# Transposing Q, K and x with the DMA crossbar instead of the matrix engine, from the third chunk on

## The chip, the cores and the metric

The kernel runs on one core of a Trainium2 chip. The metric is the device time of one execution in microseconds, as the median of three runs. The engines are named as in the profile: PE is TensorE's matmuls and PEld its weight loads, DVE is VectorE, ACT is ScalarE, POOL is GpSimd, and SP is SyncE, on whose queue the ordinary loads, the stores and (after the change) the transposing transfers are issued.

## The reference

A gated linear attention for 4 batches of 8 heads, 768 steps and 48 channels per head is followed by a mixture of four dense experts on 3,072 rows of 384 numbers:

```python
f = 1.0 / (1.0 + np.exp(-f_logit))
for t in range(S):
    state = f[:, :, t, :, None] * state + np.einsum('bhd,bhe->bhde', k[:, :, t], v[:, :, t])
    y[:, :, t] = np.einsum('bhd,bhde->bhe', q[:, :, t], state)
x = attn_out.transpose(0, 2, 1, 3).reshape(B * S, H * D)
p = domain_probs / (domain_probs.sum(-1, keepdims=True) + 1e-09)
for e in range(E):                       # E = 4, w1: 384 x 1024, w2: 1024 x 384
    h = np.maximum(x @ w1[e], 0.0)
    out += p[:, e:e + 1] * (h @ w2[e])
```

## The kernel before

**Tiling.** The 768 steps are cut into six chunks (c = 0 to 5) of 128 steps. For each chunk and each of the four batches (b), the attention part runs as a chain of steps, written here as the kernel names them with c.b behind:

- gate1, gate2 (ACT): softplus of the gates, for two batches at a time from chunk 1 on. cs (PE, L244 and L247): cumulative sums of the gates by a matmul. exps (ACT, L251 to L254): both exponentials of them.
- q, k, v: products of q and k with the exponentials (L257) and a cast of v (L261). From chunk 2 on they run on POOL alone, before that on POOL or DVE.
- tpq, tpk (PE, L265): four transposes each, of two heads at a time, into one bank of PSUM; ev_tp (L214 on DVE, tile QK) copies both to SBUF.
- at (PE, L273): eight products of K and Q, transposed; ev_at0 and ev_at1 (DVE, L277) mask them into AT.
- y (PE, L284 and L288): the chunk's output from the state and from AT; ev_y (L212 on ACT or L214 on DVE, tile yb) rounds it to bf16.
- xt (PE, L313): three transposes of yb; ev_xt (L212 or L214, tile xT) copies them into xT, the experts' input.
- kv (PE, L294), ev_kv (DVE, L301) and state (POOL, L308, L309) carry the state to the next chunk.

The experts then work on a chunk's 512 rows: h (PE, L317) is three matmuls of w1 with xT for one of eight blocks of 128 hidden units of one expert, relu (L325 on ACT or L323 on DVE) takes it out of PSUM, o (PE, L329) is four matmuls with w2, and ev_o (L336, L338) adds the result to the output tile, which store (L344) writes to memory. In chunk 1 the first two experts are done in halves of 256 rows, so an h there is three matmuls of 256 columns.

**What sets the order.** Each step is an Op with a cost per engine, a priority, the steps it depends on and the buffers it takes and frees. Plan.run places the steps one after the other on five lanes (PE, ACT, DVE, POOL, and one lane called DMA) as soon as their inputs and buffers are there by the plan's own costs, by priority. The instructions are then issued in that order on each engine, and it stays fixed: if a transfer comes later than planned, the engine that is to use it waits, and everything behind it on that engine waits too. Attention for chunk c + 1 is planned between the experts' steps for chunk c. The loads of chunk c + 2 are placed in the same stretch, on the lane DMA, which is SP's queue: SP issues loads and stores in order, and an issue that waits for its data or for its buffer holds back all those behind it.

**Buffers that matter here.** Two PSUM banks hold h's (ps_h: 2), so the third h in a row can't start until the relu of the first is done. Two buffers hold QK, two yb and two xT. Four PSUM banks (ps_t) serve all attention steps.

Of the kernel before, what the change touches and what calls it, by code (L numbers as in the profile page):

```python
# [97 lines left out]
def kernel(  # L98
# [45 lines left out]
    ones = const.tile([T, 1], BF16)  # L144
    nc.gpsimd.memset(ones, 1.0)
    pads = {}
    for nm, nb in (("gp", 2), ("qp", 1), ("kp", 1)):
# [25 lines left out]
    for nm, a in (("f", f_logit), ("q", q), ("k", k), ("v", v)):  # L173
# [12 lines left out]
    def tl(kind, *key):  # L186

        if (kind, key) not in tiles:
            room = kind if kind in rooms else "ps_t"
            slot = P.slot[(room, kind) + key if room == "ps_t" else (room,) + key]  # L190
            if room in ("gp", "qp", "kp"):
# [15 lines left out]
    def hh(b, n=1):  # L207
        return slice((b % 2) * H, (b % 2 + n) * H)
# [45 lines left out]
            nc.scalar.activation(out=tl("egs", c, b), in_=cs[0:MP, HD:HD + NP], func=AF.Exp, scale=-1.0)  # L254

    def product(c, b, j, eng):
        engines[eng].tensor_tensor(out=tl(("qp", "kp")[j], c, b)[:, 0, :, 0:D], in0=tl("qk"[j], c, b // 2)[:, hh(b), :],  # L257
                                   in1=tl("e", c, b)[:, j].rearrange("t (h d) -> t h d", d=D), op=ALU.mult)

    def cast_v(c, b, eng):  # L260
# [1 line left out]

    def pe_tp(c, b, j):
        for i in range(NP):
            nc.tensor.transpose(out=tl("tp", c, b)[:, j, i, :], in_=flat(tl(("qp", "kp")[j], c, b)[:, 0], i)[:, 0:MP],  # L265
                                identity=ident)

    def pe_at(c, b):
        QK = tl("QK", c, b)
# [10 lines left out]
    def pe_y(c, b):  # L280
        y, AT, vb, QK = tl("y", c, b), tl("AT", c, b), tl("vb", c, b), tl("QK", c, b)
        for i in range(NP):
            if c > 0:
                nc.tensor.matmul(out=y[:, i * 2 * D:(i + 1) * 2 * D], lhsT=QK[:, 0, i, :],  # L284
                                 rhs=Sb[c % 2][:, b, i, :], start=True, stop=False, skip_group_check=True)
            for r in range(2):
                h = 2 * i + r
                nc.tensor.matmul(out=y[:, h * D:(h + 1) * D], lhsT=AT[:, r, i, :], rhs=vb[:, h, :],  # L288
                                 start=(c == 0), stop=True, skip_group_check=True)

    def pe_kv(c, b):
        kp, vb = tl("kp", c, b)[:, 0], tl("vb", c, b)
        for i in range(NP):
            nc.tensor.matmul(out=tl("KV", c, b)[0:MP, i * 2 * D:(i + 1) * 2 * D], lhsT=flat(kp, i)[:, 0:MP],  # L294
                             rhs=flat(vb, i), start=True, stop=True)
# [78 lines left out]
    def attention(c, slot, gran):  # L374
        G = {}
        more = c < C - 1
        for b0 in range(0, B, gran):
            p, d, half = slot(b0, 0) - 0.5, 0.54 if gran == 1 else 0.84, b0 // 2
            g1 = P.add(f"gate1 {c}.{b0}", {"ACT": d}, lambda e, b0=b0: gate1(c, b0, gran), p,
                       deps=[ld[c, "f", b0]], takes=[("ex", c, b0)], frees=[("f", c, half)])  # L380
            g2 = P.add(f"gate2 {c}.{b0}", {"ACT": d}, lambda e, b0=b0: gate2(c, b0, gran), p + 0.1,
                       deps=[g1], takes=[("gp", c, half)], frees=[("ex", c, b0)])
            for b in range(b0, b0 + gran):
                G[b] = g2
        for b in range(B):
# [10 lines left out]
            qm = P.add(f"q {c}.{b}", pe, one(product, 0), s(4) - 0.2,  # L396
                       deps=[ex, ld[c, "q", b]], takes=[("qp", c, b)], frees=[("q", c, half), ("e", c, b)])
            km = P.add(f"k {c}.{b}", pe, one(product, 1), s(4) - 0.1,
                       deps=[ex, ld[c, "k", b]], takes=[("kp", c, b)], frees=[("k", c, half), ("e", c, b)])
            vb = P.add(f"v {c}.{b}", {"POOL": 0.5, "DVE": 0.36} if c < 2 else {"POOL": 0.5}, one(cast_v), s(4),  # L400
                       deps=[ld[c, "v", b]], takes=[("vb", c, b)], frees=[("v", c, half)])
            tq = P.add(f"tpq {c}.{b}", {"PE": 0.22}, on(pe_tp, 0), s(4), deps=[qm],
                       takes=[pt_("tp")], frees=[("qp", c, b)], lag=0.2)
            tk = P.add(f"tpk {c}.{b}", {"PE": 0.22}, on(pe_tp, 1), s(4) + 0.01, deps=[km],
                       takes=[pt_("tp")], frees=[("kp", c, b)], lag=0.2)
            et = P.add(f"ev_tp {c}.{b}", {"DVE": 0.69}, lambda e, b=b: copy(e, tl("QK", c, b), tl("tp", c, b)), s(4) + 0.1,
                       deps=[tq, tk], takes=[("QK", c, b)], frees=[pt_("tp")])
# [9 lines left out]
            xt = P.add(f"xt {c}.{b}", {"PE": 0.17}, on(pe_xt), s(13), deps=[ey],  # L417
                       takes=[pt_("xp")], frees=[("yb", c, b)], lag=0.2)
            xdone[c, b] = P.add(f"ev_xt {c}.{b}", {"ACT": 0.48, "DVE": 0.4},
                                lambda e, b=b: copy(e, tl("xT", c)[:, :, b * T:(b + 1) * T], tl("xp", c, b)),  # L420
                                s(13) + 0.1, deps=[xt], takes=[("xT", c)], frees=[pt_("xp")])
            if more:
                kv = P.add(f"kv {c}.{b}", {"PE": 0.22}, on(pe_kv), s(15), deps=[km, vb, y],
                           takes=[pt_("KV")], frees=[("vb", c, b), ("kp", c, b)], lag=0.2)
# [110 lines left out]
```

## Time and profile before

| What | Value |
|---|---|
| median of 3 runs | 324.24 us (322.96 to 326.19) |
| the profiled execution: its own time | 324.19 us |
| the profiled execution: its span | 322.5 us |
| PE busy | 306.1 us, 95% of the span |
| ACT, DVE, POOL busy | 169.1, 142.1 and 92.6 us |
| clock granted to PE | 1.00 |
| median time from issue to landing: store of 192 KB, loads of 384 KB | 1.9 us; 5.6 to 6.0 us |

The profiled execution's time lies 1.7 us above its span and within 0.05 us of the median, so the span can stand for the runs. A matmul's duration in the trace (for example 0.38 us) is longer than the distance to the next matmul's start, since they overlap; what a step costs PE is read from the distance of starts.

### The profile page before, as it was taken

What the parts mean: (1) busy time and instruction counts of PE and PEld (TensorE: products, weight loads), DVE (VectorE), ACT (ScalarE), POOL (GpSimd) and SP (SyncE); (2) the same over time, 40 slices, a digit from 0 to 9 for tenths busy, and PEclk for the clock granted to TensorE, in tenths of its full rate; (3) what the DMA queues carried; (4) which work ended last, traced back from release to release, by engine and by line L of the source; (5) the groups of instructions that cost most, each with busy time, mean ns of one, the idle gap of its engine ahead of it and who ended that gap; (6) DMA issues with size and microseconds to landing.
All of it is one profiled execution on the core that took longest, in us unless ns stands there. A gap on an engine that the chain in (4) does not pass through costs nothing.

```text
span 322.5 us, 5781 instructions
## 1 busy us (share of the span) xinstructions
PE 306.1 (95%) x2304; PEld 181.3 (56%) x2304; DVE 142.1 (44%) x271; ACT 169.1 (52%) x326; POOL 92.6 (29%) x160
## 2 busy tenths in 40 slices
PE   1979999998999999999999999999999999999995
PEld 1753455566877655555555556555555555555552
DVE  5690002399888533214653343654343543201223
ACT  5634754654767675556434455443455444465440
POOL 4695000047997800001423222423322200000000
PEclk9999999999999999999999999999999999999999
DMA  7999999999999994510400200000100000200002
GB/s 155 205 149 191 198 208 209 203 191 207 205 224 220 190 203 94 138 58 2 98 2 0 75 24 2 0 2 0 68 33 3 0 2 0 73 26 0 0 2 98
DMA packets 111531, 30.31 MB, mean 94 GB/s; under 512 B 102800, under 2 KB 109968, under 8 KB 111504
## 3 DMA queue, kind: packets, MB, share of 16 engines
q1 hardware_dynamic: 105744, 23.65, 36.7%
q0 software_dynamic: 5760, 6.29, 11.7%
q8 instruction: 18, 0.29, 0.4%
q14 instruction: 9, 0.07, 0.1%
HBM read 31.51 MB, written 4.72 MB: 112 GB/s over the span
## 4 chain that ended last, share of the span: by engine, by line
PE 89%; DVE 6%; issue 1%; ACT 1%; DMA 1%; DVEq 0%; ACTq 0%
PE ps_h L317 40%; PE ps_o L329 37%; PE ps_t L265 3%; PE ps_t L273 2%; DVE AT L277 2%; PE ps_t L288 1%; PE ps_t L244 1%; PE ps_t L313 1%; DVE kp L257 1%; PE ps_t L284 1%; PE ps_t L294 1%; PE ps_t L247 1%; DMA f<-in_f_logit_dram 1%; DVE QK L214 1%; DVE o L336 1%
## 5 line engine op out<-in xcount | busy, mean ns | idle before, releaser
L325 ACT ACTIVATE h<-ps_h 128x512 bf16<-128x512 f32 (+1 forms) x182 | 104.2, 573 | 114.1 <-PE ps_h L317 108.2
L317 PE MATMUL ps_h<-xT,w_sb 128*128 128x512 bf16 (+1 forms) x624 | 158.2, 367 | 0.7 <-ACT xT L212 0.6
L329 PE MATMUL ps_o<-w_sb,h 128*128 128x384 bf16 x768 | 154.1, 326 | 0.0
L329 PEld LDWEIGHTS <-h 128*128 128x128 bf16 x768 | 71.5, 98 | 53.1
L336 DVE SCALAR_TENSOR_TENSOR o<-ps_o,pn,o 128x384 f32<-128x384 f32 x72 | 44.4, 616 | 103.5 <-PE ps_o L329 102.3
L317 PEld LDWEIGHTS <-w_sb 128*128 128x128 bf16 x624 | 60.1, 99 | 49.2 <-issue 4.6
L277 DVE TENSOR_TENSOR AT<-ps_t,mask 128x512 bf16<-128x512 f32 x48 | 31.1, 684 | 19.9 <-PE ps_t L273 19.7
L261 POOL CAST vb<-v 128x384 bf16<-128x384 f32 x20 | 10.5, 539 | 90.5 <-PE ps_t L294 47.9
L257 POOL TENSOR_TENSOR qp<-q,e 128x384 bf16<-128x384 f32 x21 | 21.2, 1014 | 40.8 <-ACT e L251 37.1
L308 POOL TENSOR_TENSOR Sf<-Sf,egs 48x192 f32<-48x192 f32 x40 | 20.3, 508 | 20.5 <-DVE Sf L301 18.6
L323 DVE TENSOR_SCALAR h<-ps_h 128x512 bf16<-128x512 f32 (+1 forms) x26 | 14.9, 577 | 20.2 <-PE ps_h L317 15.3
L214 DVE COPY QK<-ps_t 112x1024 bf16<-112x1024 bf16 x24 | 16.5, 686 | 16.5 <-PE ps_t L265 16.5
L257 POOL TENSOR_TENSOR kp<-k,e 128x384 bf16<-128x384 f32 x19 | 19.2, 1014 | 5.2 <-ACT egs L254 4.1
L301 DVE TENSOR_TENSOR Sf<-Sf,ps_t 48x192 f32<-48x192 f32 x40 | 14.0, 349 | 6.7 <-PE ps_t L294 6.0
L338 ACT ACTIVATE o<-ps_o,pn 128x384 f32<-128x384 f32 x23 | 13.4, 581 | 5.8 <-PE ps_o L329 5.3
L251 ACT ACTIVATE e<-ps_t 128x384 f32<-128x384 f32 x24 | 11.8, 491 | 7.4 <-DVE AT L277 3.4
L309 POOL CAST sb<-Sf 48x192 bf16<-48x192 f32 x40 | 13.6, 339 | 2.6
L288 PE MATMUL ps_t<-vb,AT 128*128 128x48 bf16 x192 | 12.5, 190 | 1.5 <-DVE AT L277 1.4
L244 PE MATMUL ps_t<-gp,Ub 128*128 128x384 bf16 x24 | 8.5, 355 | 5.4 <-ACT gp L240 4.9
L288 PEld LDWEIGHTS <-AT 128*128 128x128 bf16 x192 | 10.5, 101 | 3.7 <-DVE AT L277 2.1
L265 PE MATMUL ps_t<-ident,kp 128*112 128x128 bf16 x96 | 10.4, 236 | 2.2 <-DVE kp L257 2.2
L252 ACT ACTIVATE e<-ps_t 128x384 f32<-128x384 f32 x24 | 11.8, 494 | 0.0
(48 smaller groups left out, 182.3 us busy)
## 6 DMA issues: line engine op xcount, KB each, us to landing
w_sb<-in_moe_w_dram POOLq DMA_DIRECT2D x8, 768.0 KB, 21.5
out_dram<-o SPq DMA_DIRECT2D x24, 192.0 KB, 1.9
k<-in_k_dram SPq DMA_DIRECT2D x10, 384.0 KB, 5.6
f<-in_f_logit_dram SPq DMA_DIRECT2D x10, 384.0 KB, 5.8
q<-in_q_dram SPq DMA_DIRECT2D x10, 384.0 KB, 5.8
v<-in_v_dram SPq DMA_DIRECT2D x10, 384.0 KB, 6.0
f<-in_f_logit_dram SPq DMA_DIRECT2D x4, 192.0 KB, 3.7
k<-in_k_dram SPq DMA_DIRECT2D x4, 192.0 KB, 3.9
```

Of the source, the lines that this page charges most:

```text
L214: engines[eng].tensor_copy(out=out, in_=in_)
L257: engines[eng].tensor_tensor(out=tl(("qp", "kp")[j], c, b)[:, 0, :, 0:D], in0=tl("qk"[j], c, b // 2)[:, hh(b), :], in1=tl("e", c, b)[:, j] ...
L265: nc.tensor.transpose(out=tl("tp", c, b)[:, j, i, :], in_=flat(tl(("qp", "kp")[j], c, b)[:, 0], i)[:, 0:MP], identity=ident)
L277: nc.vector.tensor_tensor(out=tl("AT", c, b)[:, r].rearrange("s i t -> s (i t)"), in0=tl("A", c, b, r).rearrange("s i t -> s (i t)"), in1= ...
L288: nc.tensor.matmul(out=y[:, h * D:(h + 1) * D], lhsT=AT[:, r, i, :], rhs=vb[:, h, :], start=(c == 0), stop=True, skip_group_check=True)
L301: nc.vector.tensor_tensor(out=Sf[rows, b], in0=Sf[rows, b], in1=KV[rows, :, r, :], op=ALU.add)
L308: nc.gpsimd.tensor_tensor(out=Sf[rows, b], in0=Sf[rows, b], in1=eg, op=ALU.mult)
L317: nc.tensor.matmul(out=tl("ps_h", c, e, fc, n0)[:, n0:n1], lhsT=w1_sb[:, e, kk, fc * 128:(fc + 1) * 128], rhs=tl("xT", c)[:, kk, n0:n1], s ...
L323: nc.vector.tensor_relu(out=dst, in_=src)
L325: nc.scalar.activation(out=dst, in_=src, func=AF.Relu)
L329: nc.tensor.matmul(out=tl("ps_o", c, e, nt)[:, 0:Din], lhsT=tl("h", c, e)[:, fc, nt * T:(nt + 1) * T], rhs=w2_sb[:, e, fc, :], start=(fc = ...
L336: nc.vector.scalar_tensor_tensor(out=o, in0=op, scalar=pe, in1=o, op0=ALU.mult, op1=ALU.add)
```

## The change

From chunk 2 on (16 of the 24 pairs of chunk and batch) the steps tpq, tpk and ev_tp become one step tp: a transposing transfer on SP's queue that reads the products of q and k (128 x 1024 bf16, 256 KB) from one SBUF tile and writes QK. The steps xt and ev_xt become one transposing transfer of 96 KB from yb into xT. For this, q's and k's products share a tile (qk, 7 of them, in place of 6 qp and 7 kp), and QK has 128 partitions in place of 112. Chunks 0 and 1 keep PE's transposes. The plan is given the new steps on the lane DMA, with a cost of 1.8 and 0.9 and 2.2 more until they count as landed.

```diff
-    rooms = {"ps_h": 2, "ps_o": 2, "ps_t": 4, "f": 4, "q": 4, "k": 4, "v": 4, "ex": 2, "gp": 4, "e": 2, "qp": 6, "kp": 7,
+    rooms = {"ps_h": 2, "ps_o": 2, "ps_t": 4, "f": 4, "q": 4, "k": 4, "v": 4, "ex": 2, "gp": 4, "e": 2, "qk": 7,
...
+    def dma_tp(c, b):
+        nc.sync.dma_start_transpose(out=tl("QK", c, b).rearrange("m j i t -> m (j i) t"),
+                                    in_=tl("qk", c, b).rearrange("t j h d -> t (j h d)"))
+
+    def dma_xt(c, b):
+        nc.sync.dma_start_transpose(out=tl("xT", c)[:, :, b * T:(b + 1) * T], in_=tl("yb", c, b))
...
+            if c < 2:
+                tq = P.add(f"tpq {c}.{b}", {"PE": 0.22}, on(pe_tp, 0), s(4), deps=[qm],
+                           takes=[pt_("tp")], frees=[("qk", c, b)], lag=0.2)
...
+            else:
+                et = P.add(f"tp {c}.{b}", {"DMA": 1.8}, on(dma_tp), s(4), deps=[qm, km], takes=[("QK", c, b)],
+                           frees=[("qk", c, b)], lag=2.2)
...
+            else:
+                xdone[c, b] = P.add(f"xt {c}.{b}", {"DMA": 0.9}, on(dma_xt), s(13), deps=[ey], takes=[("xT", c)],
+                                    frees=[("yb", c, b)], lag=2.2)
```

With the new steps and costs the plan comes out in another order. Two places matter for what follows. The line numbers of the changed kernel are seven higher from L317 on (h is L324, o is L336, the store is L351).

The first is PE in the experts' half-width stretch of chunk 1, while the attention of chunk 2 is under way. In the kernel before, two h's (in tiles 1573 and 1579) stand in a row, and then comes an attention step, cs:

```order
L317 LDWEIGHTS w_sb
L317 MATMUL ps_h_1573<-xT_927,w_sb 128x256
L317 LDWEIGHTS w_sb
L317 MATMUL ps_h_1579<-xT_927,w_sb 128x256
L317 LDWEIGHTS w_sb
L317 MATMUL ps_h_1579<-xT_927,w_sb 128x256
L317 LDWEIGHTS w_sb
L317 MATMUL ps_h_1579<-xT_927,w_sb 128x256
L244 LDWEIGHTS Ub
L244 MATMUL ps_t_1585<-gp_88,Ub 128x384
```

In the changed kernel the middle of one of its runs of four h's (1349, 1353, 1360, 1366) reads:

```order
L324 LDWEIGHTS w_sb
L324 MATMUL ps_h_1353<-xT_915,w_sb 128x256
L324 LDWEIGHTS w_sb
L324 MATMUL ps_h_1360<-xT_915,w_sb 128x256
L324 LDWEIGHTS w_sb
L324 MATMUL ps_h_1360<-xT_915,w_sb 128x256
L324 LDWEIGHTS w_sb
L324 MATMUL ps_h_1360<-xT_915,w_sb 128x256
L324 LDWEIGHTS w_sb
L324 MATMUL ps_h_1366<-xT_915,w_sb 128x256
```

The transposes that stood between h's are gone and the attention steps that hang on them have moved later. Behind chunk 1's last xt the kernel before has no place with three h's in a row; the changed one has three runs of four.

The second place is SP's queue in the second half of the program. Before, only stores stand there (chunk 3's, then chunk 4's):

```order
L344 DMA out_dram<-o_2603 128x384
L344 DMA out_dram<-o_2636 128x384
L344 DMA out_dram<-o_2684 128x384
L344 DMA out_dram<-o_2725 128x384
L344 DMA out_dram<-o_3198 128x384
L344 DMA out_dram<-o_3231 128x384
```

In the changed kernel the transposing transfers of chunk 5 (QK and xT) stand between chunk 3's last two stores and chunk 4's first:

```order
L269 DMA_TRANSPOSE QK_2953<-qk_104 128x8x128
L351 DMA out_dram<-o_2566 128x384
L351 DMA out_dram<-o_2602 128x384
L269 DMA_TRANSPOSE QK_3029<-qk_92 128x8x128
L273 DMA_TRANSPOSE xT_3089<-yb_3080 128x3x128
L269 DMA_TRANSPOSE QK_3114<-qk_94 128x8x128
L273 DMA_TRANSPOSE xT_3089<-yb_3173 128x3x128
L269 DMA_TRANSPOSE QK_3203<-qk_96 128x8x128
L273 DMA_TRANSPOSE xT_3089<-yb_3255 128x3x128
L273 DMA_TRANSPOSE xT_3089<-yb_3336 128x3x128
L351 DMA out_dram<-o_3021 128x384
```

Each of these transfers now stands in one line with stores that wait for ev_o, and with loads in the stretch before; what they feed (at and h on PE) stands where the plan put it.

More of the change, by code (lines that the diff above doesn't have):

```diff
@@ L146 @@
     pads = {}
-    for nm, nb in (("gp", 2), ("qp", 1), ("kp", 1)):
+    for nm, nb in (("gp", 2), ("qk", 2)):
         for i in range(rooms[nm]):
@@ L190, in tl @@
             slot = P.slot[(room, kind) + key if room == "ps_t" else (room,) + key]
-            if room in ("gp", "qp", "kp"):
+            if room in ("gp", "qk"):
                 tiles[kind, key] = pads[room, slot]
@@ L256, in product @@
     def product(c, b, j, eng):
-        engines[eng].tensor_tensor(out=tl(("qp", "kp")[j], c, b)[:, 0, :, 0:D], in0=tl("qk"[j], c, b // 2)[:, hh(b), :],
+        engines[eng].tensor_tensor(out=tl("qk", c, b)[:, j, :, 0:D], in0=tl("qk"[j], c, b // 2)[:, hh(b), :],
                                    in1=tl("e", c, b)[:, j].rearrange("t (h d) -> t h d", d=D), op=ALU.mult)
@@ L264, in pe_tp @@
         for i in range(NP):
-            nc.tensor.transpose(out=tl("tp", c, b)[:, j, i, :], in_=flat(tl(("qp", "kp")[j], c, b)[:, 0], i)[:, 0:MP],
+            nc.tensor.transpose(out=tl("tp", c, b)[:, j, i, :], in_=flat(tl("qk", c, b)[:, j], i)[:, 0:MP],
                                 identity=ident)
+    def dma_tp(c, b):
[3 more added lines that the diff above has]
+        nc.sync.dma_start_transpose(out=tl("xT", c)[:, :, b * T:(b + 1) * T], in_=tl("yb", c, b))
     def pe_at(c, b):
@@ L283, in pe_y @@
             if c > 0:
-                nc.tensor.matmul(out=y[:, i * 2 * D:(i + 1) * 2 * D], lhsT=QK[:, 0, i, :],
+                nc.tensor.matmul(out=y[:, i * 2 * D:(i + 1) * 2 * D], lhsT=QK[0:MP, 0, i, :],
                                  rhs=Sb[c % 2][:, b, i, :], start=True, stop=False, skip_group_check=True)
@@ L396, in attention @@
             qm = P.add(f"q {c}.{b}", pe, one(product, 0), s(4) - 0.2,
[L397 removed]
+                       deps=[ex, ld[c, "q", b]], takes=[("qk", c, b)], frees=[("q", c, half), ("e", c, b)])
             km = P.add(f"k {c}.{b}", pe, one(product, 1), s(4) - 0.1,
[L399 removed]
+                       deps=[ex, ld[c, "k", b]], takes=[("qk", c, b)], frees=[("k", c, half), ("e", c, b)])
             vb = P.add(f"v {c}.{b}", {"POOL": 0.5, "DVE": 0.36} if c < 2 else {"POOL": 0.5}, one(cast_v), s(4),
                        deps=[ld[c, "v", b]], takes=[("vb", c, b)], frees=[("v", c, half)])
[L402 to L407, printed above, removed]
+            if c < 2:
+                tq = P.add(f"tpq {c}.{b}", {"PE": 0.22}, on(pe_tp, 0), s(4), deps=[qm],
+                           takes=[pt_("tp")], frees=[("qk", c, b)], lag=0.2)
+                tk = P.add(f"tpk {c}.{b}", {"PE": 0.22}, on(pe_tp, 1), s(4) + 0.01, deps=[km],
+                           takes=[pt_("tp")], frees=[("qk", c, b)], lag=0.2)
+                et = P.add(f"ev_tp {c}.{b}", {"DVE": 0.69}, lambda e, b=b: copy(e, tl("QK", c, b)[0:MP], tl("tp", c, b)), s(4) + 0.1,
+                           deps=[tq, tk], takes=[("QK", c, b)], frees=[pt_("tp")])
+            else:
+                et = P.add(f"tp {c}.{b}", {"DMA": 1.8}, on(dma_tp), s(4), deps=[qm, km], takes=[("QK", c, b)],
+                           frees=[("qk", c, b)], lag=2.2)
             at = P.add(f"at {c}.{b}", {"PE": 0.35}, on(pe_at), s(7), deps=[et],
@@ L416, in attention @@
                        deps=[y], takes=[("yb", c, b)], frees=[pt_("y")])
[L417 to L421, printed above, removed]
+            if c < 2:
+                xt = P.add(f"xt {c}.{b}", {"PE": 0.17}, on(pe_xt), s(13), deps=[ey],
+                           takes=[pt_("xp")], frees=[("yb", c, b)], lag=0.2)
+                xdone[c, b] = P.add(f"ev_xt {c}.{b}", {"ACT": 0.48, "DVE": 0.4},
+                                    lambda e, b=b: copy(e, tl("xT", c)[:, :, b * T:(b + 1) * T], tl("xp", c, b)),
+                                    s(13) + 0.1, deps=[xt], takes=[("xT", c)], frees=[pt_("xp")])
+            else:
+                xdone[c, b] = P.add(f"xt {c}.{b}", {"DMA": 0.9}, on(dma_xt), s(13), deps=[ey], takes=[("xT", c)],
+                                    frees=[("yb", c, b)], lag=2.2)
             if more:
                 kv = P.add(f"kv {c}.{b}", {"PE": 0.22}, on(pe_kv), s(15), deps=[km, vb, y],
-                           takes=[pt_("KV")], frees=[("vb", c, b), ("kp", c, b)], lag=0.2)
+                           takes=[pt_("KV")], frees=[("vb", c, b), ("qk", c, b)], lag=0.2)
                 ek = P.add(f"ev_kv {c}.{b}", {"DVE": 0.74}, on(ev_kv), s(15) + 0.1,
```

4 lines of the change are left out of this document (2 added, 2 removed).

## The prediction

> **What bounds the kernel now.** I read the page's engine lines and the shares of the chain that ended last, then the busy times by stretch (behind the stretch's length: PE, PEld, DVE, ACT and POOL busy, with instructions in brackets, then PE's clock, the DMA engines' share, GB/s).
>
> ```profile
> PE 306.1 (95%) x2304; PEld 181.3 (56%) x2304; DVE 142.1 (44%) x271; ACT 169.1 (52%) x326; POOL 92.6 (29%) x160
> ...
> DMA  7999999999999994510400200000100000200002
> ...
> q1 hardware_dynamic: 105744, 23.65, 36.7%
> ...
> PE 89%; DVE 6%; issue 1%; ACT 1%; DMA 1%; DVEq 0%; ACTq 0%
> ```
>
> ```profile
> 80.00:92.00 12.00, 12.00 (x166) 9.95 (x164) 10.50 (x22) 9.15 (x27) 11.37 (x19) 1.00 1.03 206
> 92.00:104.00 12.00, 12.00 (x154) 9.48 (x152) 10.51 (x23) 8.26 (x20) 9.38 (x21) 1.00 1.06 223
> 104.00:116.00 12.00, 12.00 (x105) 7.91 (x104) 6.90 (x12) 7.73 (x17) 7.44 (x11) 1.00 1.17 198
> ...
> 228.00:275.00 47.00, 47.00 (x349) 26.41 (x347) 20.01 (x33) 22.72 (x42) 7.82 (x8) 1.00 0.05 18
> ```
>
> PE is busy 306.1 of 322.5 us at full clock, carries 89% of the chain, and in the stretches where the change acts it is busy for the whole of them. DVE and ACT, which lose copies by the change, are not full there, so what they lose is worth nothing by itself; PE's time is. The DMA engines are full up to about 125 us and nearly idle behind that, so the new transfers first meet loads and later an empty queue.
>
> **What is removed.** The starts on PE in one batch of chunk 4 show what a transpose costs it:
>
> ```profile
> 198.52 0.81 PE L317 MATMUL ps_h<-xT,w_sb 128*128 128x512 bf16 x3
> 199.17 0.39 PE L265 MATMUL ps_t<-ident,qp 128*112 128x128 bf16 x4
> 199.39 0.39 PE L265 MATMUL ps_t<-ident,kp 128*112 128x128 bf16 x4
> 199.61 0.81 PE L329 MATMUL ps_o<-w_sb,h 128*128 128x384 bf16 x4
> ...
> 200.91 0.36 PE L294 MATMUL ps_t<-vb,kp 128*112 128x96 bf16 x4
> 201.11 0.33 PE L244 MATMUL ps_t<-gp,Ub 128*128 128x384 bf16 x1
> ```
>
> ```profile
> 267.03 0.81 PE L329 MATMUL ps_o<-w_sb,h 128*128 128x384 bf16 x4
> 267.30 0.56 DVE L214 CAST yb<-ps_t 128x384 bf16<-128x384 f32 x1 [0.48 <-PE ps_t L288]
> ...
> 269.62 0.33 PE L313 MATMUL ps_t<-ident,yb 128*128 128x128 bf16 x3
> ...
> 269.79 0.81 PE L329 MATMUL ps_o<-w_sb,h 128*128 128x384 bf16 x4
> ...
> 271.74 0.81 PE L317 MATMUL ps_h<-xT,w_sb 128*128 128x512 bf16 x3
> ```
>
> The transposes of Q and K occupy PE from 199.17 to 199.61, 0.44 us; those of x from 269.62 to 269.79, 0.17 us. Per batch that is 0.61 us, and for 16 batches **9.8 us**, all of it on a PE that has other work ready, so all of it is gained unless PE then waits.
>
> **What is added on PE's side: waits for relu.** The kernel has two tiles for h, so a third h in a row waits for the first's relu. After the change three runs of four h's stand in chunk 1's half-width stretch, where there were none. Chunk 0's h's, all in a row, show the price, and a later pair with an o behind it shows the pace without it:
>
> ```profile
> 31.27 1.46 PE ps_h L317 x6
> 32.76 1.46 PE ps_h L317 x6
> ...
> 117.53 1.29 PE ps_h L317 x6
> ```
>
> ```profile
> L325 ACT ACTIVATE h<-ps_h 128x512 bf16<-128x512 f32 x161 | 96.2, 597 | 108.6 <-PE ps_h L317 102.7 <-DVE o L336 3.0 <-DVE Sf L301 0.9
> ...
> L325 ACT ACTIVATE h<-ps_h 128x256 bf16<-128x256 f32 x21 | 8.0, 385 | 5.5 <-PE ps_h L317 5.5
> ...
> L323 DVE TENSOR_SCALAR h<-ps_h 128x256 bf16<-128x256 f32 x11 | 4.6, 422 | 2.8 <-PE ps_h L317 2.6
> ...
> L251 ACT ACTIVATE e<-ps_t 128x384 f32<-128x384 f32 x24 | 11.8, 491 | 7.4 <-DVE AT L277 3.4 <-PE ps_t L247 2.9 <-DVE vb L261 0.9
> ```
>
> ```profile
> 103.93 0.49 PE L317 MATMUL ps_h<-xT,w_sb 128*128 128x256 bf16 x3
> 104.26 0.81 PE L329 MATMUL ps_o<-w_sb,h 128*128 128x384 bf16 x4
> ```
>
> A pair takes 32.76 - 31.27 = 1.49 us there instead of 1.29, a wait of 0.20. It is the relu (0.60) and the matmul's tail and handoffs (0.25) less the next h (0.65). With half the width, h takes 104.26 - 103.93 = 0.33 and relu 0.39 to 0.42, so a wait is 0.39 + 0.25 - 0.33 = 0.3 us; where ACT or DVE is in the middle of another instruction (an exponential, 0.49), up to 0.8. Three runs cost 0.9 to 2.4 us; I take 1.8, since by the windows above DVE is busy for 88% and ACT for 69 to 76% of the stretch from 80 to 104. If relu is always at hand, the cost is nothing.
>
> **What is added: 32 transfers.** PE waits only where a transfer lands later than the place that the fixed order gives its user, so what counts is the cover, the time from a transfer's release to its user.
>
> For xT the tightest place is the chunk's last batch, and the rows above show it for chunk 5: DVE has rounded yb at 267.30 + 0.56 = 267.86, and the next chunk's first h starts at 271.74, or at 271.57 without the 0.17 of transposes. Cover: **3.7 us**. At the turns to chunks 4 and 3 a kv, or a kv and an o, stands there besides, and at the turn to chunk 2 seven o's do.
>
> For QK in chunk 5 these rows count:
>
> ```profile
> 234.34 0.81 PE L329 MATMUL ps_o<-w_sb,h 128*128 128x384 bf16 x4
> ...
> 236.38 1.00 POOL L257 TENSOR_TENSOR kp<-k,e 128x384 bf16<-128x384 f32 x1
> ...
> 244.94 0.40 PE L273 MATMUL ps_t<-QK 48*128 48x128 bf16 x8
> ```
>
> The product of k is ready at 237.38 and its user starts at 244.94, less 0.44 of transposes: 7.1 us of cover, and the other batches of chunk 5 are ordered alike. In chunk 2 it is less, because there are two QK buffers: the transfer of batch 2 waits for y of batch 0, and between that y and the user there now stand three o's and four h's (0.65 each by the starts above, 4.55), one kv (201.11 - 200.91 = 0.20) and one at (0.40 with its tail), 5.0 us or more, **4.8 us** less the handoff. The order has two such places, and up to six more in chunks 2 and 3 whose transfers stand behind loads or stores.
>
> The trace has no transposing transfer, so its price is bounded by other transfers on SP's queue (bytes and time from issue to landing):
>
> ```profile
> out_dram<-o SPq DMA_DIRECT2D x4, 192.0 KB, 2.1
> ...
> q<-in_q_dram SPq DMA_DIRECT2D x1, 384.0 KB, 3.7
> k<-in_k_dram SPq DMA_DIRECT2D x1, 384.0 KB, 4.3
> ```
>
> ```profile
> out_dram<-o SPq DMA_DIRECT2D x8, 192.0 KB, 1.8
> ```
>
> ```profile
> k<-in_k_dram SPq DMA_DIRECT2D x3, 384.0 KB, 6.1
> ```
>
> A store of 192 KB on an empty queue lands in 1.8 us, a load of 384 KB with little before it in 3.7 to 4.3, and a load behind others in 6.1. QK's 256 KB lie between: bounds 1.8 and 6.1; by size alone, between the store and a free load of 4.0, it is 2.5. I take 3.5, nearer to the load, since the loads too move short pieces (the page's queue q1: 23.65 MB in 105,744 packets, 224 bytes each). For xT (96 KB) the bounds are 1.8 and 4.3, since by then little else is in flight, and I take 2.5. Neither exceeds its cover, so these waits are put at **0**. If they land later by e than their covers, PE loses e at each place: two to four turns for xT, about eight places for QK.
>
> [...]
>
> **What moves past SP's queue.** A load or store behind a transfer whose product or buffer is late must wait too. These rows show the room:
>
> ```profile
> 97.02 2.65 SPq L344 DMA_DIRECT2D out_dram<-o  x1
> ...
> 119.70 1.65 SPq L218 DMA_DIRECT2D v<-in_v_dram  x1
> 131.18 0.36 SPq L344 DMA_DIRECT2D out_dram<-o  x1
> ```
>
> ```profile
> 111.44 0.83 ACT L236 ACTIVATE ex<-f 128x768 f32<-128x768 f32 x1
> ```
>
> The fourth store of chunk 0 and the loads behind it were issued from 97.02 on, the last burst at 119.70, and then SP stood still till 131.18. So the loads of chunks 4 and 5 may slip by 10 us; their first user (the gates, at 111.44 and later) runs one chunk ahead of need. In the other direction, a QK of chunk 5 stands behind two stores of chunk 3: the second's o is on PE at 234.34 for 0.81 us in the rows above, so it ends two microseconds before the product of k is ready at 237.4. Both are put at 0.
>
> **Sum.** The profiled execution took 324.2 us (1.7 above its span, and the median of the runs is the same): 324.2 - 9.8 + 1.8 + 0 = **316.2 us**. The start (up to 80 us) and the end (from 275 us, the last expert stages) have no edit in them.
>
> **The rivals.**
>
> *1. Transfers as slow as loads in a full queue (slower).* Mechanism: a transposing transfer lands like a load behind others, QK in 6.1 us and xT in 4.3. For it: in the stretch to 125 us the queue is full and is served in order. Against it: behind 160 us nothing else is in flight. Price: QK exceeds 4.8 by 1.3 at eight places, 10.4; xT exceeds 3.7 by 0.6 at the last two turns, 1.2. Time: 316.2 + 11.6 = 328. It decides from a QK landing of 4.8 + 8.0/8 = 5.8 us on; there the gain of 8.0 is gone.
>
> *2. The gain is eaten (no change).* QK lands in about 5.4 us and the relu waits reach their upper end of 2.4: 324.2 - 9.8 + 2.4 + 8 x 0.6 = 321.6. The bounds of 1.8 to 6.1 allow it and no row excludes it; the room for it is narrow, half a microsecond of landing time.
>
> *3. A transfer that works block by block (much slower).* QK is eight blocks of 128 x 128; if each were handled after the one before it, the landing could be twice that of a load in a full queue, 12.2 us. That exceeds 4.8 at eight places and 7.1 at the other eight, 59 + 41 = 100 us, so about 416. Against it: loads of short packets land in 3.7 to 4.3. [...]
>
> *4. No relu waits, quick transfers.* 314.4.
>
> **How the numbers follow.** About 1% (3.2 us) is what a measurement of this kernel can tell from no change. Forecast and rival 4 together 0.65 (314 to 319), rival 2 0.13, rival 1 0.15, rival 3 0.07. Faster 0.65, same 0.13, slower 0.22. The likeliest case's own range is 314 to 319; to leave out no more than 2 in 10 the range runs from 314 to 330, past rival 1's 328, with rival 3 left out.
>
> **What would show it.** L265 falls from 192 to 64 matmuls and L313 (L320) from 72 to 24. Issue to landing for QK is under 4.8 and for xT under 3.7 us. PE's idle before L273 (L280) and before h at a chunk's turn stays near 0, and new idle on PE before h between 85 and 105 us, released by relu, sums to 1 to 3 us. I am wrong if PE waits for DMA before L280: then the landing times say which rival it was.

## The result and the profile after

The changed kernel took **315.63 us** (median, 315.22 to 315.96) against 323.78 us of the kernel before on the same chip: a ratio of 0.974, with a 95% interval of 0.968 to 0.979. The forecast was 316.2. The profiled execution of after took 315.96 us, its span is 314.1.

The page of after, in the lines that were shown of before (engines' busy time, the DMA engines' busy tenths, SP's transfer queue, the chain's shares):

```profile
PE 295.3 (94%) x2098; PEld 171.1 (54%) x2128; DVE 132.5 (42%) x249; ACT 163.0 (52%) x310; POOL 92.6 (29%) x160
...
DMA  8999999999999087999692113200322200200002
...
q1 hardware_dynamic: 129296, 29.42, 49.2%
...
PE 88%; DVE 7%; issue 2%; ACT 1%; DMA 1%; DVEq 0%; ACTq 0%
```

PE is busy for 10.8 us less than before and still carries 88% of the chain. The new transfers show in q1: 5.8 MB more, in 23,552 more packets. The DMA engines now stay busy to the 21st of the 40 slices (165 us), where they had little to do from the 16th on; in between, the 14th slice (102 to 110 us) has become empty.

The groups of instructions by shape (line, engine, operation, tiles | busy, mean ns of one | idle time of the engine before them and what ended it), and below them the DMA issues (KB where known, median us from issue to landing):

```profile
L324 PE MATMUL ps_h<-xT,w_sb 128*128 128x512 bf16 x498 | 140.5, 385 | 2.2 <-ACT xT L212 0.6 <-issue 0.2
...
L280 PE MATMUL ps_t<-QK 48*128 48x128 bf16 x192 | 10.6, 233 | 1.0 <-DVE QK L214 0.4 <-DVE yb L214 0.4 <-DVE Sf L308 0.2
...
L265 PE MATMUL ps_t<-ident,qk 128*112 128x128 bf16 x64 | 7.2, 268 | 3.5 <-DVE qk L257 2.7 <-ACT xT L212 0.6 <-ACT e L252 0.2
...
L320 PE MATMUL ps_t<-ident,yb 128*128 128x128 bf16 x24 | 3.3, 260 | 0.5 <-DVE QK L214 0.2 <-ACT yb L212 0.2
```

```profile
QK<-qk SPq DMA_TRANSPOSE x16, 3.2
xT<-yb SPq DMA_TRANSPOSE x16, 2.4
```

L265 fell to 64 and L320 to 24 instructions, as announced. PE's idle time before the products that read QK (L280) and before h (L324) is ended by DVE and ACT; no DMA is named. Q and K's transfer lands in 3.2 us, x's in 2.4 (medians; the slowest of the 16 in 4.4 and 3.9).

The turn to chunk 5 in the timeline (start, duration), which the prediction used for x's cover, and the first and the last of the three runs of four h's in chunk 1 (x12 matmuls, or x6 and x6):

```profile
259.02 0.56 DVE L214 CAST yb<-ps_t 128x384 bf16<-128x384 f32 x1 [0.47 <-PE ps_t L295]
...
259.61 1.18 SPq L273 DMA_TRANSPOSE xT<-yb  x1
...
263.31 0.81 PE L324 MATMUL ps_h<-xT,w_sb 128*128 128x512 bf16 x3
```

```profile
90.69 1.82 PE L324 MATMUL ps_h<-xT,w_sb 128*128 128x256 bf16 x12
92.35 1.46 PE L336 MATMUL ps_o<-w_sb,h 128*128 128x384 bf16 x8
...
100.23 0.82 PE L324 MATMUL ps_h<-xT,w_sb 128*128 128x256 bf16 x6
101.44 0.81 PE L324 MATMUL ps_h<-xT,w_sb 128*128 128x256 bf16 x6 [0.39 <-DVE h L330]
102.09 1.46 PE L336 MATMUL ps_o<-w_sb,h 128*128 128x384 bf16 x8
```

yb is ready at 259.58, the transfer lands at 262.0 (2.4 later), and h starts at 263.31: 1.3 us to spare. The same h stood at 271.74 before, so 8.4 us are gained up to here, which is the whole gain: 9.8 of transposes less what the runs of h cost. Up to 82 us PE's order is the same in both kernels, and this execution of after happens to be 0.3 us behind there (82.03 against 81.75 at the last weight loads that are the same), so behind that point the change gives 8.7. The runs took 92.35 - 90.69 = 1.66 (the second as much) and 102.09 - 100.23 = 1.86 us for four h's of 0.33, that is 0.34, 0.34 and 0.54 too much, 1.2 us together.

### The profile page after: what moved, and what is told of

It reads as the page before. It is cut to its first block, busy times and chain, and to the rows that moved or that the text cites. A ratio compares the mean times of both kernels' runs of the same rounds, so it can differ in the third digit from the quotient of the medians.

```text
span 314.1 us, 5415 instructions
## 1 busy us (share of the span) xinstructions
PE 295.3 (94%) x2098; PEld 171.1 (54%) x2128; DVE 132.5 (42%) x249; ACT 163.0 (52%) x310; POOL 92.6 (29%) x160
## 4 chain that ended last, share of the span: by engine, by line
PE 88%; DVE 7%; issue 2%; ACT 1%; DMA 1%; DVEq 0%; ACTq 0%
PE ps_h L324 40%; PE ps_o L336 39%; PE ps_t L280 2%; DVE qk L257 2%; DVE AT L284 2%; PE ps_t L295 1%; PE ps_t L244 1%; PE ps_t L291 1%; PE ps_t L301 1%; PE ps_t L247 1%; DMA f<-in_f_logit_dram 1%; PE ps_t L265 1%; DVE QK L214 1%; DVE o L343 1%; DVE vb L261 1%
## 5 line engine op out<-in xcount | busy, mean ns | idle before, releaser
L332 ACT ACTIVATE h<-ps_h 128x512 bf16<-128x512 f32 (+1 forms) x176 | 101.7, 579 | 111.2 <-PE ps_h L324 104.1
L324 PE MATMUL ps_h<-xT,w_sb 128*128 128x512 bf16 (+1 forms) x594 | 154.0, 367 | 2.9 <-ACT xT L212 0.6
L336 PE MATMUL ps_o<-w_sb,h 128*128 128x384 bf16 x768 | 153.0, 326 | 0.2
L336 PEld LDWEIGHTS <-h 128*128 128x128 bf16 x768 | 72.0, 98 | 56.8
L324 PEld LDWEIGHTS <-w_sb 128*128 128x128 bf16 x624 | 60.5, 99 | 50.9 <-issue 6.5
L261 POOL CAST vb<-v 128x384 bf16<-128x384 f32 x20 | 10.7, 537 | 72.9 <-DMA v<-in_v_dram 36.5
L257 POOL TENSOR_TENSOR qk<-q,e 128x384 bf16<-128x384 f32 x21 | 21.2, 1014 | 30.2 <-ACT e L251 29.9
L330 DVE TENSOR_SCALAR h<-ps_h 128x256 bf16<-128x256 f32 (+1 forms) x32 | 17.4, 549 | 23.6 <-PE ps_h L324 23.2
L257 POOL TENSOR_TENSOR qk<-k,e 128x384 bf16<-128x384 f32 x19 | 19.3, 1015 | 21.8 <-ACT egs L254 11.3
L214 DVE CAST yb<-ps_t 128x384 bf16<-128x384 f32 x17 | 9.5, 556 | 13.8 <-PE ps_t L295 12.4
L244 PE MATMUL ps_t<-gp,Ub 128*128 128x384 bf16 x24 | 8.5, 355 | 5.4 <-ACT gp L240 4.9
L236 ACT ACTIVATE ex<-f 128x768 f32<-128x768 f32 (+1 forms) x14 | 10.5, 753 | 1.9 <-DMA f<-in_f_logit_dram 1.7
```

The source lines that it names most:

```text
L257: engines[eng].tensor_tensor(out=tl("qk", c, b)[:, j, :, 0:D], in0=tl("qk"[j], c, b // 2)[:, hh(b), :], in1=tl("e", c, b)[:, j].rearrange( ...
L261: engines[eng].tensor_copy(out=tl("vb", c, b), in_=tl("v", c, b // 2)[:, hh(b), :])
L324: nc.tensor.matmul(out=tl("ps_h", c, e, fc, n0)[:, n0:n1], lhsT=w1_sb[:, e, kk, fc * 128:(fc + 1) * 128], rhs=tl("xT", c)[:, kk, n0:n1], s ...
L330: nc.vector.tensor_relu(out=dst, in_=src)
L332: nc.scalar.activation(out=dst, in_=src, func=AF.Relu)
L336: nc.tensor.matmul(out=tl("ps_o", c, e, nt)[:, 0:Din], lhsT=tl("h", c, e)[:, fc, nt * T:(nt + 1) * T], rhs=w2_sb[:, e, fc, :], start=(fc = ...
```

## The experiments

All times are medians, and ratios are against the kernel before, run on the same chip. One thing has to be known to read differences of under 1 us: up to the 200th weight load, which no edit of these touches, executions of the same instructions differ. That load starts 37.7 us after the first in the profiled execution of after, and between 36.5 and 37.3 in the five experiments `none`, `quiet`, `latex`, `lateq` and `relu`. Where PE's order is the same, I therefore compare the starts of the weight loads one by one and say what changes behind that point.

**What do the transfers cost as they are?** In `none` they are left out, and PE reads constant tiles in place of QK and xT:

```diff
-        nc.sync.dma_start_transpose(out=tl("QK", c, b).rearrange("m j i t -> m (j i) t"),
-                                    in_=tl("qk", c, b).rearrange("t j h d -> t (j h d)"))
+        tl("QK", c, b)
...
-        nc.sync.dma_start_transpose(out=tl("xT", c)[:, :, b * T:(b + 1) * T], in_=tl("yb", c, b))
+        tl("xT", c)
```

> The 32 transposing transfers are left out: from chunk 2 on, QK and xT are tiles that are set to zero once, so at, y and h read zeros; all else is as in the changed kernel, in the same order. By my theory the transfers cost PE nothing as they are: 315.0 to 315.8. Rival C (the transfers slow something that the trace does not show as a wait, by contention or by holding SP's loads): 313.5 or less.

Measured: 315.00 us, ratio 0.974 (0.973 to 0.976). The weight loads of the two kernels keep the same distance, to 0.01 us, from the 200th to the last; the 0.77 us between the profiled executions arise ahead of any transfer. The 32 transfers cost nothing.

**What is each half worth?** `qk` transposes only Q and K by DMA, `x` only x; in each the other half keeps PE's branch in every chunk.

```diff
-            if c < 2:          # x's branch in qk, Q and K's branch in x
+            if c < 6:
```

> Only Q and K go by the transposing transfer; x is transposed on TensorE as before, in every chunk. Theory (each removed PE instruction gives back its PE time, the transfers stay hidden, and where three or more first-matmul blocks h follow each other at half width PE waits for the relus): 323.4 - 16 x 0.44 = 316.4, plus about 1.3 for the runs of h, which this order has as well (six blocks that are third in a row or later): 317.7, between 317.2 and 318.3. Rival A (the runs of h came from x's transposes leaving PE): no relu waits here, 316.4. Rival B (TensorE transposes cost more than their own time, through the PSUM copies that DVE no longer makes): 315 or less.

> Only x goes by the transposing transfer; Q and K are transposed on TensorE in every chunk. Theory: 323.4 - 16 x 0.17 = 320.7, and no runs of h in this order (none is third in a row), so nothing comes on top: 320.4 to 321.0. Rival A (the relu waits come with x's part): 322. Rival B (x's path sets the chunk turns, so taking TensorE and ACT out of it gives more than its 2.7): below 320.

Measured: `qk` 317.54 us (ratio 0.980, 0.976 to 0.985), `x` 320.99 us (0.990, 0.987 to 0.994), before 323.83. The halves gave 6.3 and 2.8 us where 5.7 and 2.7 were worked out. `qk` has runs of four h's like after, `x` has none, so these runs come with Q and K's part. Behind the 200th weight load the profiled executions of `qk`, `x` and after are 6.0, 2.8 and 8.7 us shorter than that of before; the transposes less 1.2 us for the runs of h give 5.8, 2.7 and 8.6.

**Are the runs of h slowed by relu?** In `relu` the relus of the half-width stretch write 16 columns instead of 256:

```diff
+        m1 = n0 + 16 if c == 1 and e < 2 else n1
-        dst, src = tl("h", c, e)[:, fc, n0:n1], tl("ps_h", c, e, fc, n0)[:, n0:n1]
+        dst, src = tl("h", c, e)[:, fc, n0:m1], tl("ps_h", c, e, fc, n0)[:, n0:m1]
...
+            lhsT=(w1_sb[:, e, 0, nt * T:(nt + 1) * T] if c == 1 and e < 2 else tl("h", c, e)[...])
```

> After, but in the half-width stretch of chunk 1 each relu writes 16 columns instead of 256, and the second matmul there reads a slice of the first weights in place of h (part of the second chunk's output is left out; PE's order, its instructions and shapes are the same). Theory (in the runs of four h's PE waits for a relu to free one of two PSUM buffers; the three runs took 1.3 us more than so many matmuls elsewhere): 315.6 - 1.3 = 314.3, and each run of twelve h matmuls takes 1.30 us from its start to the next instruction's instead of 1.66. Rival (matmuls of 256 columns in a row are slower by themselves, since each weight load has less work to hide behind): no change, 315.6.

Measured: 314.52 us, ratio 0.972 (0.970 to 0.975). The groups of `relu` and its timeline:

```profile
L331 DVE TENSOR_SCALAR h<-ps_h 128x16 bf16<-128x16 f32 x17 | 2.8, 172 | 9.4 <-PE ps_h L324 9.3
L333 ACT ACTIVATE h<-ps_h 128x16 bf16<-128x16 f32 x15 | 2.8, 184 | 6.8 <-PE ps_h L324 6.5
```

```profile
89.97 1.58 PE L324 MATMUL ps_h<-xT,w_sb 128*128 128x256 bf16 x12
91.39 1.46 PE L337 MATMUL ps_o<-w_sb 128*128 128x384 bf16 x8
```

The run shown now takes 1.42 us instead of 1.66, the second as well, and the third 1.61 instead of 1.86; the weight loads behind gain 0.74 us at this place and nowhere else behind the start (another 0.7 arises in the start). So PE did wait for relu. It isn't all: 0.10 per run (0.29 in the third) remains with a relu of 0.17 to 0.18 us, which is the prediction's rule again: 0.18 + 0.25 - 0.33 = 0.10. In the third run DVE comes to its relu late in both kernels, because it is still at ev_o (L347, from 100.44 for 0.62 us in after). The 1.3 us that my expectation gave back entirely contained this rest.

**How much room do the transfers have?** `late1` puts one scratch transposing transfer of the same size ahead of each of the 32, `late2` two:

```diff
+    def scratch(src, n):
+        for i in range(1):                  # 2 in late2
+            junk[0] += 1
+            nc.sync.dma_start_transpose(out=junks[junk[0] % 4][:, 0:n, :], in_=src)
     def dma_tp(c, b):
+        scratch(tl("qk", c, b).rearrange("t j h d -> t (j h d)"), 8)
...
     def dma_xt(c, b):
+        scratch(tl("yb", c, b), 3)
```

> One transposing transfer of the same source into a scratch tile is issued ahead of each of the 32 (nothing is left out). SP's queue holds each for 1.2 us, so QK lands about 3.2 + 1.2 = 4.4 us after its release and xT about 2.4 + 1.2 = 3.6. By my theory PE waits only beyond the covers of 4.8 and 3.7, so the time stays within 1.5 us of the changed kernel's 315.6: 315.5 to 317. Rival A (the covers are much larger than I worked out): 315.6 here, and the same with two scratch transfers. Rival B (no cover is left, each of 32 transfers is waited for): 16 places times 1.2 us, 335.

> Two scratch transfers ahead of each of the 32. QK lands about 5.7 us after its release and xT 4.8. By my theory QK exceeds its cover of 4.8 by 0.9 at up to eight places and xT its 3.7 to 4.6 by 0.2 to 1.1 at three turns: 5 to 10 us more than the changed kernel, 320 to 326, and the trace shows PE waiting for DMA before L280 or L324 at those places. Rival A (covers much larger): 316 or less. Rival B (each one waited for): 350 or more.

Measured: `late1` 327.37 us against 323.42 before (ratio 1.011, 1.007 to 1.015), `late2` 356.25 us (1.101, 1.099 to 1.104). Both expectations failed, by 10 us and by 30. The list of PE's waits in `late2` (us in total, times, longest), and Q and K's transfer among its DMA issues:

```profile
PE ps_h L332 <- DMA xT<-yb: 16.6, 4, 9.3
...
PE ps_t L288 <- DMA QK<-qk: 7.2, 5, 2.4
```

```profile
QK<-qk SPq DMA_TRANSPOSE x16, 3.3
```

PE now waits for transfers that land, once issued, as fast as ever. They are issued late: each transposing transfer holds SP for 1.2 us, and the next stands behind it. By the weight loads, `late1` loses its time at five places: 1.6 us before a product that reads QK in chunk 2, 4.5 at the turn to chunk 2 and 5.3 at the turn to chunk 3 (both before the first h and shortly behind it), 0.9 before an h between them, and 0.5 in chunk 5.

So my next theory was that the room is short only where loads and stores share SP's queue. `quiet` has the scratch in chunks 4 and 5 alone, `latex` ahead of x's transfers alone, `lateq` ahead of Q and K's alone:

```diff
     def dma_tp(c, b):
+        if c >= 4:                          # quiet; left out in latex
+            scratch(tl("qk", c, b).rearrange("t j h d -> t (j h d)"), 8)
...
     def dma_xt(c, b):
+        if c >= 4:                          # quiet; left out in lateq
+            scratch(tl("yb", c, b), 3)
```

> After with one scratch transposing transfer ahead of each of Q/K's and x's, but only in the last two chunks (16 scratch transfers instead of 32), where no loads are left on SP's queue. Theory (one scratch everywhere cost 11.7 us because at the turns to the third and fourth chunk the transfers stand in line behind loads and stores on SP, and not because the cover is everywhere used up): the 1.2 us that a scratch holds SP for is hidden here, 315.6 to 316.4. Rival (the cover is short everywhere): half of 11.7, so 321.5.

> After with one scratch transposing transfer ahead of each of x's alone (16 scratch transfers, in all four last chunks). One scratch ahead of all 32 cost 11.7 us over after: 8.4 us at the turns to the third and fourth chunk, before the first h that reads xT, and 3 us before the products that read QK. Theory (at these turns the last x transfer of the chunk stands on SP behind its own scratch, loads and stores): nearly all of the 8.4 us comes back with x's scratch alone: 321 to 325. Rival (the scratch ahead of Q/K's delays the chain from QK to y, and x's transfer is late because y is late): 315.6 to 317 here.

> After with one scratch transposing transfer ahead of each of Q/K's alone. Theory (as in the run with x's alone): the cover of 4.8 us less the 3.2 us that the transfer takes leaves 1.6 us, more than the 1.2 us that a scratch holds SP, but the turns' x transfers stand behind some of it: 316 to 319. Rival (Q/K's scratch makes y late at the turns): 321 to 325.

Measured: `quiet` 314.86 us (ratio 0.972, 0.968 to 0.976), `latex` 321.41 (0.992, 0.990 to 0.994), `lateq` 316.28 (0.978, 0.976 to 0.980). The 16 scratch transfers of `quiet` cost 0.1 us behind the start. In chunks 4 and 5 the transfers have 1.2 us to spare, as the rows of the turn to chunk 5 say (1.3). `latex` loses 6.1 us at the turn to chunk 2 and only 0.8 at the turn to chunk 3; `lateq` 0.9 in all. The 5.3 us of `late1` at the turn to chunk 3 thus need both scratches. SP's queue at the turn to chunk 2, first of after, then of `latex`:

```profile
121.21 1.29 SPq L218 DMA_DIRECT2D v<-in_v_dram  x1
122.54 1.47 SPq L218 DMA_DIRECT2D f<-in_f_logit_dram  x1
124.98 1.72 SPq L273 DMA_TRANSPOSE xT<-yb  x1
```

```profile
123.33 1.25 SPq L219 DMA_DIRECT2D v<-in_v_dram  x1
124.62 1.58 SPq L219 DMA_DIRECT2D f<-in_f_logit_dram  x1
126.30 2.94 SPq L272 DMA_TRANSPOSE junk<-yb  x1
129.28 1.25 SPq L280 DMA_TRANSPOSE xT<-yb  x1
```

and PE there, after and `latex`:

```profile
129.27 0.81 PE L336 MATMUL ps_o<-w_sb,h 128*128 128x384 bf16 x4
...
129.92 1.46 PE L324 MATMUL ps_h<-xT,w_sb 128*128 128x512 bf16 x5
...
134.87 0.34 PE L280 MATMUL ps_t<-QK 48*128 48x128 bf16 x6
```

```profile
128.07 0.81 PE L343 MATMUL ps_o<-w_sb,h 128*128 128x384 bf16 x4
132.07 0.58 PE L331 MATMUL ps_h<-xT,w_sb 128*128 128x512 bf16 x1 [3.19 <-issue]
...
134.58 1.48 PE L343 MATMUL ps_o<-w_sb,h 128*128 128x384 bf16 x4
135.86 1.48 PE L331 MATMUL ps_h<-xT,w_sb 128*128 128x512 bf16 x3
...
139.75 0.40 PE L287 MATMUL ps_t<-QK 48*128 48x128 bf16 x8
```

In after, x's last transfer is issued at 124.98, as soon as yb is ready, behind three loads of 384 KB (the rows show two, a load of q stands ahead of them), lands 3.6 us later at 128.6, and h reads it at 129.92: 1.3 us to spare. In `latex` yb is ready at 123.75, but the loads have themselves been pushed back by the scratch before and hold SP until 126.2, and then the scratch holds it for 2.94 us instead of 1.2; the transfer is issued at 129.28, 5.5 us after yb, and lands 2.7 later. Before this, `latex` was 129.27 - 128.07 = 1.20 us ahead, and at the next product 139.75 - 134.87 = 4.88 us behind: 6.1 us lost. PE stands from 128.7 (the end of the o's of 128.07, at 0.65 us) to 132.07. That is 3.4 us; the other 2.7 come behind it: the four o matmuls of 134.58 take 135.86 - 134.58 = 1.28 us instead of 0.65. The busy times by stretch of `latex` (PE, PEld, DVE, ACT, POOL, PE's clock, DMA share, GB/s) show why:

```profile
130.00:133.00 3.00, 0.71 (x2) 0.41 (x4) 0.00 (x0) 1.69 (x2) 2.78 (x5) 0.64 0.67 107
133.00:136.00 3.00, 3.00 (x9) 1.19 (x9) 1.38 (x2) 0.94 (x3) 3.00 (x4) 0.50 1.19 295
136.00:139.00 3.00, 3.00 (x13) 1.28 (x12) 0.62 (x1) 0.71 (x2) 1.46 (x3) 0.73 1.02 213
```

The granted clock is 0.64, 0.50 and 0.73 there, and 1.00 before 130 and from 139 on. If it had no values but 1.00 and 0.50, these means put it at 0.50 from 130.8 to 137.6 (an estimate from the rows): it fell some 2 us into the wait and came back some 5.5 us after PE had work again. This wait of 3.4 us on PE is paid nearly twice (6.1 us).

**Could the transfers start a chunk earlier?** In `c1` both branches begin with chunk 1:

```diff
-            if c < 2:          # both places
+            if c < 1:
```

> The transfers begin one chunk earlier, with the second chunk, while weights and loads still fill the DMA engines (their mean busy share there is 1.0 to 1.2 of the 16 engines' span). Theory (the gain rests on DMA engines and an SP queue with room): 4 x 0.61 = 2.4 us of PE work goes, but transfers land 5 us and more after issue and wait in line on SP, and PE waits for them: 320 to 340. Rival (the transfers hide anywhere): 315.6 - 2.4 = 313.2.

Measured: 333.87 us, ratio 1.031 (1.026 to 1.035). PE's waits, and the busy times of the stretch in which the first of these transfers land and of the one before it:

```profile
PE ps_t L244 <- ACT gp L240: 11.4, 4, 4.8
PE ps_t L280 <- DMA QK<-qk: 4.2, 2, 3.4
PE ps_h L324 <- DMA xT<-yb: 3.1, 2, 2.2
```

```profile
68.00:80.00 12.00, 6.08 (x51) 4.21 (x49) 3.77 (x6) 7.08 (x17) 7.86 (x9) 0.82 1.30 211
80.00:92.00 12.00, 5.77 (x69) 4.42 (x68) 5.62 (x11) 5.47 (x15) 7.88 (x14) 0.50 1.03 175
```

The time is as expected, the way to it only in part. Transfers that PE waits for cost 4.2 + 3.1 us. Another 6.5 us goes to cs (L244), which waits 11.4 us for gates against 4.9 in after, and more to a clock of 0.50. By the mean of 0.82 from 68 to 80 that clock begins at about 75.7 us (an estimate, as in `latex`), during a wait of cs of 4.7 us that lasts until 78.8, and the first of these transfers is issued only at 78.5. So the order alone, in which the plan places chunk 1's steps later when they go by transfer, has a part in the loss; how much of the 18 us is the order and how much the queue stays open.

**Is there a better order?** `ld` plans all loads 10% and the weights 25% cheaper; `ld2` plans only the loads of chunk 2 and later cheaper (1.7 instead of 2.1 for two batches), and Q and K's transfer at 1.3 instead of 1.8. The work is that of after.

```diff
-        op = P.add(f"ld {nm}{c}.{b}", {"DMA": 1.05 * n}, lambda e: load(c, nm, b, n), prio,
+        op = P.add(f"ld {nm}{c}.{b}", {"DMA": 0.95 * n}, lambda e: load(c, nm, b, n), prio,                     # ld
-        wd[e, which] = wd[i] = P.add(f"w {i}", {"DMA": 4.8}, lambda _: None, -500 + i, deps=[iss], lag=2.0)
+        wd[e, which] = wd[i] = P.add(f"w {i}", {"DMA": 3.6}, lambda _: None, -500 + i, deps=[iss], lag=2.0)       # ld
+        op = P.add(f"ld {nm}{c}.{b}", {"DMA": (1.05 if c < 2 else 0.85) * n}, lambda e: load(c, nm, b, n), prio,  # ld2
```

> The changed kernel with the plan's cost of a load lowered from 2.1 to 1.9 per two batches and of a weight transfer from 4.8 to 3.6, nearer to what the traces show; the work is the same, the order is another, in which the attention of chunks 1 and 2 stands earlier and two of the three runs of four h's go. By my theory the changed kernel loses 1.3 us in these runs and the plan holds PE's attention steps back for transfers that have long landed: 309.5 to 313. Rival D (PE is full whatever the order): 314.5 to 316.

> After with two costs of the plan changed, which moves the order from 77 us on and leaves the first chunk's alone: a load of the third and later chunks is planned at 1.7 us of the DMA queue instead of 2.1, and Q/K's transfer at 1.3 instead of 1.8. The work is the same. Theory (the run with cheaper loads everywhere lost in the first 68 us, where its order put the second chunk's work ahead of its loads and weights, and the runs of h's at half width cost about 0.35 us each): here the first part stays, and two h's stand third in a row or later instead of six, so 0.7 to 1.4 us fewer: 314.0 to 315.0. Rival (any order that plans loads faster than they are ends in waits for data, from 100 us on too): 317 to 320.

Measured: `ld` 319.70 us (ratio 0.989, 0.986 to 0.992), `ld2` 316.22 (0.976, 0.974 to 0.978). Neither beats after, and both missed what was expected of them, `ld` by 7 us and `ld2` by 1. In `ld` PE stands 3.2 us for gates whose load is late and 1.8 for weights; the timeline of it and the list of `ld2`'s waits:

```profile
57.10 0.84 ACT L236 ACTIVATE ex<-f 128x768 f32<-128x768 f32 x1 [4.05 <-DMA f<-in_f_logit_dram]
...
58.87 0.32 PE L244 MATMUL ps_t<-gp,Ub 128*128 128x384 bf16 x1 [3.21 <-ACT gp L240]
```

```profile
PE ps_h L324 <- ACT h L332: 1.8, 3, 1.1
...
PE ps_t L280 <- DMA QK<-qk: 0.9, 1, 0.9
```

In `ld2` the runs of four are gone, but three h's still wait for relu, 1.8 us in all: 0.3 at half width (93.05 us), and 1.1 (121.64) and 0.4 at full width, so the new order has such waits elsewhere. And a product waits 0.9 us for QK; that the earlier order brought it closer to its transfer is likely, but not shown.

## Why the prediction was right

**PE's transposes, -9.8.** Right. The halves measured apart gave 6.3 and 2.8 us, and behind the start they and after itself come out within 0.2 of the transposes less the runs of h (6.0, 2.8 and 8.7 against 5.8, 2.7 and 8.6).

**The relu waits, +1.8.** The mechanism was right, shown by `relu`, and the term was 0.6 too large: the trace has 1.2. The rule of 0.3 us a wait held (0.34 in two runs). I chose a value between the bounds because DVE was busy for 88% of that stretch before; in after it is busy there for 69 and 46% (8.30 and 5.50 of 12 us), and only the third run cost more than the rule says. The nearer end, 0.9, would have been the better choice. That the forecast came within 0.6 of the result doesn't measure this: 0.4 of it is the starting value (324.2, where the median beside the result is 323.78), and the gain itself, 8.0 forecast and 8.15 measured, is met to 0.2, closer than the start varies from one execution to the next. So close a hit is luck; the terms are what was tested.

```profile
80.00:92.00 12.00, 11.86 (x129) 9.37 (x128) 8.30 (x20) 9.07 (x25) 11.36 (x19) 1.00 1.00 205
92.00:104.00 12.00, 11.47 (x90) 8.29 (x89) 5.50 (x12) 7.36 (x18) 6.62 (x9) 1.00 0.95 202
```

**The transfers, 0.** Right, shown by `none`. I took 3.5 us for QK's landing and 2.5 for x's; the trace has medians of 3.2 and 2.4, so rivals 1 and 2 fell by their own conditions (5.8 and 5.4).

**Rival 3, block by block.** It needed a landing of 12.2 us, and QK's took 3.2. QK's eight blocks land 0.8 us after what x's three need, so a block costs about 0.16 us and a transfer about 1.9 in any case (both estimates, worked out from the medians of 3.2 and 2.4).

**The covers.** This is the step that failed, although the sum doesn't show it. I worked out 3.7 us at the turn to chunk 5, which held, and took the other turns to be safer because more PE work stands there. At the turn to chunk 2 the cover is longer, 4.9 us by the rows above, but the transfer stands behind three loads and needs 3.6, so that no more than 1.3 us is left. I had compared a landing on a free queue with a cover on a full one. The turns to chunks 3 and 4 have 1.5 and 1.6 us left, so the room is about the same at all four; what differs is how much later one more transfer ahead of each makes them start, 1.2 us where SP is free and 5.5 at the turn to chunk 2 (`latex`). The runs with scratch transfers show what that meant: one more ahead of each turns a gain of 8 us into a loss of 4. That `late1` (327.4) comes out at rival 1's 328 is chance: its transfers land as fast as ever once issued (medians of 3.3 and 2.4 us), and the time is lost because SP issues them late.

**What moves past SP's queue, 0.** Right in the sum, but not in the working: SP's last loads weren't at 119.70. The rows of before, then of after, for the last load of f:

```profile
131.63 0.38 SPq L218 DMA_DIRECT2D f<-in_f_logit_dram  x1
```

```profile
146.62 1.71 SPq L218 DMA_DIRECT2D f<-in_f_logit_dram  x1
```

It is issued 15 us later than before. That is more than the 10 us that I allowed, and PE still doesn't wait for it. In `none`, which has the new order but no transfers, the same load is issued at 141.1, so some 10 us of the slip come with the order and some 5 with the transfers. These hold the queue not only while they are issued: one of Q and K's that must wait for its buffer, until PE has done an earlier y, keeps everything behind it waiting too. The waits of SP's queue for this in after (us in total, times, longest):

```profile
SPq L269 <- PE ps_t L295: 29.2, 6, 7.9
```

The longest, up to 108.96, is the empty slice in the DMA engines' line of after.

## What to carry to other kernels

Where one engine bounds the kernel, as PE did here (busy for 95% of the span), work that it hands to a DMA queue can be worth its time on that engine (here 9.8 us of transposes, of which 8.7 were gained behind 82 us), provided the fixed order leaves each transfer its landing time on the queue as it is at that place (3.6 us behind three loads, where the median is 2.4). So measure the room before building on it: a scratch transfer ahead of each real one shows within one run where it is short (`late1`, at five places). And a wait of a few microseconds on PE can cost more than its length, where the clock falls (3.4 us cost 6.1 in `latex`).

## What the hardware showed that I had not expected

A transposing transfer holds SP for 1.2 us whether it moves 256 or 96 KB (instruction durations on SP, minimum, median and maximum):

```profile
L269 SPq DMA_TRANSPOSE QK<-qk x16: 1231/1233/2138, 94.0 to 246.5; - x16
```

```profile
L273 SPq DMA_TRANSPOSE xT<-yb x16: 1178/1214/1907, 110.3 to 259.6; - x16
```

By these medians 32 of them take 39 us of SP's queue. Single holds are longer, 2.9 us behind loads in `latex`; but one of 2.1 us in after, at 190.79, has no load near it, so what lengthens them stays open.

PE's clock fell with short waits: in `latex` (above) with one of 3.4 us, and in `late1` to a mean of 0.55 from 135 to 138 us, behind one of 2.6 us that ended at 133.24:

```profile
PE ps_h L332 <- DMA xT<-yb: 2.6, 1, 2.6
```

```profile
129.00:132.00 3.00, 1.60 (x13) 0.95 (x12) 1.24 (x2) 0.32 (x2) 1.75 (x4) 1.00 1.32 170
132.00:135.00 3.00, 1.76 (x7) 0.78 (x7) 0.69 (x1) 2.16 (x4) 2.86 (x5) 0.88 0.79 171
135.00:138.00 3.00, 3.00 (x11) 1.25 (x10) 0.69 (x1) 0.90 (x4) 3.00 (x4) 0.55 1.12 251
138.00:141.00 3.00, 3.00 (x25) 1.68 (x24) 1.31 (x2) 2.10 (x6) 0.76 (x2) 1.00 1.04 225
```

Worked out from these means as in `latex`, it was at 0.50 from 134.3 to 137.7, for 3.4 us, and in `latex` for 6.8 (both estimates). But in `ld` a wait of 3.2 us (up to 58.87, above), longer than that of `late1`, wasn't enough: the clock stayed at 1.00 there and behind it.

```profile
56.00:68.00 12.00, 9.13 (x82) 5.32 (x82) 7.65 (x13) 6.92 (x15) 4.59 (x5) 1.00 1.14 207
```

So the length of the wait alone didn't decide it in these runs; what did isn't shown.
